# Block sums in four and three operations instead of five and four, and the first chunk's products of probabilities and v in one call

## The chip, the cores and the metric

The kernel runs on one core of a Trainium2 chip. The metric is the time of one execution in microseconds (us) of the device. TensorE (PE) multiplies matrices, with its weight loads shown apart (PEld); VectorE (DVE), ScalarE (ACT) and GpSimd (POOL) do the arithmetic around them; SyncE (SP) issues the DMAs.

## The reference

A transformer block on x of 2048 tokens by 448: layer norm, attention with 16 heads of 28 in which each token sees itself and the 255 tokens before it, a residual addition, a second layer norm, and a gated feed-forward layer of width 1792 with a second addition. All is float32.

```python
h  = x + attention(layernorm(x)) @ wo          # q.k scaled by 28**-0.5, window of 256
g  = layernorm(h) @ w_gate                     # [2048, 448] @ [448, 1792]
u  = layernorm(h) @ w_up
h2 = h + (gelu(g) * u) @ w_down
```

## The kernel before

**Precision.** Nearly every matrix operand is split in two: `to_hi` (L390, ScalarE) rounds it into a float32r part, `to_lo` (L393, VectorE or GpSimd) subtracts that part from the original. TensorE then multiplies hi by hi, hi by lo and lo by hi. L390 and L393 are helpers, so in the profile all splits have these two lines, and the tile tells them apart.

**Order of the work.** Nothing runs in the order in which it is written. Each operation is recorded with an engine, an assumed cost, a key and its dependencies (`Lists.op`); at the end `Lists.run` walks through an assumed time, takes for each engine the ready operation of the lowest key, and so fixes the order in which every engine issues its instructions. The constants at the top (LAG_T, LAG_P, EDGE, CKEY, XLATE, WLATE and so on) are offsets of keys; XADD, XADD2, XLO, XLO2, WLO and WLO2 say which of VectorE and GpSimd does a given sum or split. A changed constant can therefore move instructions anywhere.

**Attention (to about 316 us).** Tokens go in four chunks of 512, and heads in four groups of four, which makes 16 blocks B. Projections of q, k and v are L672 and L618; scores for the row maxima are L723 (with L727 on VectorE), scores again for the probabilities L798, their exponential L802 (ScalarE), the masks at the edges of the window L817 (GpSimd, `select`). `attend` (L826) multiplies v with the probabilities, in four column tiles of TensorE (L836); its matmuls are issued without a break, per call. A block has six tiles m of 128 keys, of which the first chunk (c = 0, blocks 0 to 3) has the last four. Lines 1653 to 1657 call it twice per block, with tiles (0, 1, 2) and (3, 4, 5), and in the first chunk (2, 3) and (4, 5). The output projection is L894, its addition L897.

**Feed-forward (from about 316 us to the end).** The first three column pairs of w_gate and w_up (CL = 3) are multiplied directly (L1131, L1143). The others go by Winograd's scheme, which makes a two-by-two block product of seven block products instead of eight, at the price of sums of blocks of the weights and of the tokens. Contraction blocks are 192 rows (three times 64) and lie in the two halves of 64 partitions, "sides" 0 and 1, so that two products run at once in the two row halves of TensorE (L1333, `both`). PRODUCT (L924) says at which side and slot the operands of a product lie; slots 0 to 2 hold sums, slot 3 plain blocks. The results are added up and gated at L1339 to L1361, and the product with w_down is L1407, added to the residual at L1424.

`weight_set(n)` (L1177) brings one weight matrix of a pair: DMAs, sums of blocks on GpSimd into the scratch tile xn (`sum_`, all at L1202), then hi and lo splits into the slots. There are 18 sets. `tokens_x(cp, ...)` (L994) does the same for the tokens, once for each half cp of the tokens, in three parts k of 64 rows: seven loads, a `fill`, four sums (L1041, L1044, L1047, L1050) into scratch tiles, then splits. In both halves L1044 is on GpSimd and the others on VectorE.

With a the blocks of a weight matrix, the five sums of a set are, on the sides named: a21 + a22 (both), a11 - a21 (both), the first minus a11 (side 0), the second plus a12 (side 1), and that minus a22 (side 1).

The final order of TensorE in the feed-forward stage is a chain in the written order (`queued`); sums and splits have only their keys.

Of the kernel before, what the change touches and what calls it, by code (L numbers as in the profile page):

```python
# [32 lines left out]
LAG_T = 5.0  # L33
VLAST = (-26, -21, 18, 28)
ELAST = 7
LAG_P = 15.5
LAG_V = 10.5
EDGE = 12
WIN = 9
# [3 lines left out]
CWL = 175  # L43
LATER = 4
ALONE = 5
CKEY = (214, 262)
CWKEY = (266, 222, 262, 330)
CHOLD = (10, 13, 12, 13)
X0KEY = 1330
XTIME = (6, 7, 8)  # L50
WFIRST = 1310
WLO2 = ('dve', 'dve', 'dve', 'pool')
XADD2 = ('dve', 'pool', 'dve', 'dve')
XLO2 = ('dve', 'dve', 'dve', 'pool', 'dve')
XLATE = 125
XSTEP = 60
HASTE = 300
OUTK = 80
WLATE = 110
UNIT = 100  # L60
XADD = ('dve', 'pool', 'dve', 'dve')
XLO = ('pool', 'dve', 'dve', 'dve', 'dve')
WLO = ('dve', 'pool', 'dve', 'dve')
DKEY = 284
# [5 lines left out]
LNLATE = 300  # L70
PKL = 2
LN1 = (-20, -14, 39, 128)
LN2 = (152, 260)
VKEY = (-27, -23, 17, 33)
# [177 lines left out]
def block_kernel(ctx: ExitStack, tc, x, wqk_in, wv_in, wo_in, gu_in, rest_in, cw_in, down_in, out):  # L252
# [4 lines left out]
    op = L.op  # L257
# [5 lines left out]
    def f(ap):  # L263
        return ap.bitcast(F32)
# [659 lines left out]
    PRODUCT = {1: (0, 0), 6: (0, 1), 7: (0, 2), 4: (0, 3), 2: (1, 0), 5: (1, 1), 3: (1, 2)}  # L924
# [69 lines left out]
    def tokens_x(cp, key, parts):  # L994
# [16 lines left out]
        def loads_x(k0, n):  # L1011
            for l, slot, side, c, row in ((1, 2, 0, c2, 192), (1, 1, 0, c2, 0), (1, 1, 1, c2, 0), (1, 0, 0, c1, 0),
                                          (1, 0, 1, c1, 192), (0, 1, 1, c1, 0), (1, 3, 0, c1, 192)):
                load(l, slot, side, c, row, k0, n)
# [20 lines left out]
        for k in parts:  # L1035
            key = key0 + (0 if cp else XSTEP * k)
            loads_x(k, 1)
            fill(k, 1, c2, 192 + 64 * k)
            if k < 2:
                fill(k, 2, 2 * cp + k, 384)  # L1040
            arith((XADD, XADD2)[cp][0], 512, key + 1, lambda e, k=k: e.tensor_tensor(  # L1041
                scratch(1, 0), f(area(1, 2, k, 0)), f(area(1, 1, k, 0)), op=OP.subtract),
                [*xtok(cp, 1, 2, k, 0), *xtok(cp, 1, 1, k, 0), *held(1)[1:]], held(1)[:1])
            arith((XADD, XADD2)[cp][1], 512, key + 1, lambda e, k=k: e.tensor_tensor(  # L1044
                scratch(0, 1), f(area(1, 1, k, 1)), f(area(0, 1, k, 1)), op=OP.subtract),
                [*xtok(cp, 1, 1, k, 1), *xtok(cp, 0, 1, k, 1), *held(0)[1:]], held(0)[:1])
            arith((XADD, XADD2)[cp][2], 512, key + 1, lambda e, k=k: e.tensor_tensor(  # L1047
                scratch(0, 0), scratch(1, 0), f(area(1, 0, k, 0)), op=OP.add),
                [*xtok(cp, 1, 0, k, 0), *held(1), *held(0)[1:]], held(0)[:1])
            arith((XADD, XADD2)[cp][3], 512, key + 1, lambda e, k=k: e.tensor_tensor(  # L1050
                scratch(2, 0), f(area(1, 3, k, 0)), scratch(0, 0), op=OP.subtract),
                [*xtok(cp, 1, 3, k, 0), *held(0), *held(2)[1:]], held(2)[:1])
            split(2, k, 2, 1)
            split(1, k, 2, 0)
            split(3, k, 2 if k < 2 else 0, 2)
            split(0, k, 2)
# [120 lines left out]
    def weight_set(n, key):  # L1177
# [28 lines left out]
        sum_(0, SE, 2, lambda: at(0, 1, 2), lambda: at(0, 2, 2), OP.add, wtok(n, 0, 1, 2) + wtok(n, 0, 2, 2))  # L1206
        sum_(384, SG, 2, lambda: at(0, 0, 2), lambda: at(0, 1, 2), OP.subtract, wtok(n, 0, 0, 2) + wtok(n, 0, 1, 2))
        sum_(0, SE, 0, sc(0, 0), lambda: at(0, 0, 0), OP.subtract, wtok(n, 0, 0, 0))
        sum_(384, SG, 1, sc(384, 1), lambda: at(1, 0, 1), OP.add, wtok(n, 1, 0, 1))
        sum_(384, SG, 1, sc(384, 1), lambda: at(0, 2, 1), OP.subtract, wtok(n, 0, 2, 1))  # L1210
# [410 lines left out]
    for c in range(CS):  # L1621
# [17 lines left out]
        for g in range(NG):  # L1639
# [13 lines left out]
            for half in ((0, 1, 2), (3, 4, 5)) if c else ((2, 3), (4, 5)):  # L1653
# [130 lines left out]
```

## Time and profile before

| | |
|---|---|
| median of 3 runs | 711.2 us (709.17 to 713.15) |
| the profiled execution | 710.19 us |
| its span, first to last instruction | 708.5 us |
| mean granted clock of TensorE | 0.998 |
| POOL L1202, sums of weights | 54 of 64x384, 36 of 128x384, 18 of 64x128 |
| L836, products with v | 352 matmuls, in the trace x704 |

A row of instructions in the profile reads: line, engine, operation, output tile <- input tiles, shapes and count; then busy time and the mean of one in ns, and then the idle time of the engine ahead of them with what ended it. In the timeline the first two numbers are the start and the duration in us. A row of the table by stretch has, for PE, PEld, DVE, ACT and POOL in this order, the busy time and the number of instructions, and then TensorE's granted clock as a share of full speed, the DMA share and GB/s. A row of waits has the total in us, how many times, and the longest.

### The profile page before, as it was taken

What the parts mean: (1) busy time and instruction counts of PE and PEld (TensorE: products, weight loads), DVE (VectorE), ACT (ScalarE), POOL (GpSimd) and SP (SyncE); (2) the same over time, 40 slices, a digit from 0 to 9 for tenths busy, and PEclk for the clock granted to TensorE, in tenths of its full rate; (3) what the DMA queues carried; (4) which work ended last, traced back from release to release, by engine and by line L of the source; (5) the groups of instructions that cost most, each with busy time, mean ns of one, the idle gap of its engine ahead of it and who ended that gap; (6) DMA issues with size and microseconds to landing.
All of it is one profiled execution on the core that took longest, in us unless ns stands there. A gap on an engine that the chain in (4) does not pass through costs nothing.

```text
span 708.5 us, 15457 instructions
## 1 busy us (share of the span) xinstructions
PE 695.2 (98%) x5544; PEld 587.3 (83%) x5544; DVE 534.5 (75%) x1228; ACT 414.7 (59%) x911; POOL 318.6 (45%) x431
## 2 busy tenths in 40 slices
PE   8999999999999999999999999999999999999997
PEld 7887788787888887778788798888899888898996
DVE  7977778888697879927586789986745966877764
ACT  7748576866686666866545455645434545546431
POOL 5613563644464346441354767633403456556100
PEclk9999999999999999999999999999999999999999
DMA  8997777887877677306885765504303553443102
GB/s 309 279 285 225 255 184 184 207 248 171 233 200 229 201 204 181 118 8 150 214 230 164 219 183 174 147 5 139 89 1 125 175 180 113 137 153 87 42 15 104
DMA packets 104692, 116.26 MB, mean 164 GB/s; under 512 B 44632, under 2 KB 82392, under 8 KB 104040
## 3 DMA queue, kind: packets, MB, share of 16 engines
q1 hardware_dynamic: 104472, 115.17, 56.5%
q8 instruction: 43, 0.70, 0.4%
q14 instruction: 33, 0.27, 0.1%
q10 hardware_dynamic: 144, 0.11, 0.0%
HBM read 84.97 MB, written 44.47 MB: 183 GB/s over the span
## 4 chain that ended last, share of the span: by engine, by line
PE 89%; DVE 6%; ACT 2%; issue 1%; DMA 1%; POOL 1%; DVEq 0%; ACTq 0%
PE bank L1333 24%; PE bank L1407 17%; PE bank L672 9%; PE bank L798 7%; PE bank L723 7%; PE bank L1131 7%; PE bank L836 6%; PE bank L894 5%; PE bank L618 5%; PE bank L1143 2%; DVE xT L393 1%; DVE hres L1424 1%; DVE proj L393 1%; DVE v L1343 1%; PE bank L448 0%
## 5 line engine op out<-in xcount | busy, mean ns | idle before, releaser
L727 DVE CUSTOM_DVE_ANT_0 mt<-bank,mt 128x384 bf16<-128x384 f32 (+2 forms) x256 | 127.6, 526 | 25.8 <-PE bank L723 23.0
L802 ACT ACTIVATE pp<-bank 128x384 f32<-128x384 f32 (+1 forms) x212 | 104.4, 534 | 27.1 <-PE bank L798 18.0
L817 POOL TENSOR_SCALAR_AFFINE_SELECT pp<-pp 128x512 f32<-128x512 f32 x120 | 75.8, 646 | 83.9 <-ACT pp L802 81.6
L672 PE MATMUL bank<-xT 128*128 128x512 f32 x308 | 95.4, 399 | 0.0
L1333 PE MATMUL bank<-xT,proj 64*128 64x512 f32 x735 | 94.9, 388 | 0.0
L1333 PEld LDWEIGHTS bank<-xT,proj 64*128 64x128 f32 x735 | 75.8, 184 | 9.1 <-DVE v L1343 0.3
L798 PE MATMUL bank<-rq,rk 104*128 104x384 f32 (+2 forms) x352 | 82.1, 306 | 0.5 <-ACT pp L802 0.4
L723 PE MATMUL bank<-rk,rq 84*128 84x384 f32 (+2 forms) x256 | 80.8, 340 | 0.0
L1407 PE MATMUL bank<-proj,gh 64*128 64x448 f32 x624 | 73.0, 364 | 1.5 <-ACT e L1253 0.9
L798 PEld LDWEIGHTS bank<-rq,rk 104*128 104x128 f32 x352 | 58.9, 189 | 15.0 <-ACT pp L802 4.5
L1407 PEld LDWEIGHTS bank<-proj,gh 64*128 64x128 f32 x624 | 61.3, 186 | 7.8 <-ACT e L1253 1.7
L1424 DVE TENSOR_TENSOR hres<-bank,hres 128x448 f32<-128x448 f32 (+1 forms) x113 | 62.7, 609 | 5.5 <-PE bank L1407 5.5
L1253 ACT ACTIVATE e<-bank 1x1 f32<-1x1 f32 x139 | 21.8, 157 | 74.9 <-PE bank L1407 52.7
L672 PEld LDWEIGHTS bank<-xT 128*128 128x128 f32 x308 | 55.8, 189 | 7.2 <-DVE proj L393 0.5
L1202 POOL TENSOR_TENSOR xn<-proj 128x384 f32<-128x384 f32 (+1 forms) x36 | 34.1, 952 | 56.1 <-DMA proj<-gu 36.0
L723 PEld LDWEIGHTS bank<-rk,rq 84*128 84x128 f32 x256 | 47.0, 189 | 9.8 <-issue 1.9
L393 DVE TENSOR_TENSOR proj<-proj 128x448 fp32r<-128x448 f32 (+2 forms) x42 | 34.2, 820 | 24.5 <-ACT proj L390 23.9
L1333 PE MATMUL bank<-xo,proj 64*128 64x512 f32 x366 | 49.6, 399 | 1.2 <-ACT e L1253 1.0
L390 ACT ACTIVATE rq<-bank 8x512 fp32r<-8x512 f32 x64 | 37.6, 588 | 21.3 <-PE bank L754 20.2
L618 PE MATMUL bank<-proj,xT 128*128 128x448 f32 (+1 forms) x220 | 48.9, 333 | 0.0
L836 PE MATMUL bank<-pp,v 128*29 128x384 f32 (+2 forms) x704 | 45.2, 388 | 0.0
L1333 PEld LDWEIGHTS bank<-xo,proj 64*128 64x128 f32 x366 | 38.5, 189 | 7.2 <-ACT e L1253 1.6
(177 smaller groups left out, 1429.5 us busy)
## 6 DMA issues: line engine op xcount, KB each, us to landing
rk<-k SPq DMA_DIRECT2D x44, 336.0 KB
rq<-q SPq DMA_DIRECT2D x32, 336.0 KB
gu<-in_gu_dram SPq DMA_DIRECT2D x18, 480.0 KB
proj<-gu SPq DMA_DIRECT2D x24, 288.0 KB
q<-proj SPq DMA_DIRECT2D x12, 448.0 KB
proj<-down SPq DMA_DIRECT2D x22, 224.0 KB
proj<-gu SPq DMA_DIRECT2D x24, 192.0 KB
k<-proj SPq DMA_DIRECT2D x9, 448.0 KB
```

The source lines that it names most:

```text
L618: op("pe", mm(224 * n), 0.29 if n == 1 else 0.38, key + a / 16, lambda a=a, h=h, wb=wb, xb=xb: nc.tensor.matmul(bank[b.k][:, 0:224 * n], x ...
L672: op("pe", mm(512) + 0.002, 0.403, key, lambda a=a, h=h, wb=wb, xb=xb: nc.tensor.matmul(bank[b.k], wqk[m][:, h, wb, :], xT[:, xb, cc * 128 ...
L723: nc.tensor.matmul(bank[b.k][:, o:384], rq[u][0:3 * DH, j, i * 128:i * 128 + 128], rk[u][0:3 * DH, j, m0 * 128:(i + 3) * 128], start=True, ...
L727: nc.vector.tensor_tensor_reduce(junk[s % 2][:, o:384], bank[b.k][:, o:384], mask[:, o:384], 1.0, -BIG, OP.add, OP.max, mx[:, i, j:j + 1])
L798: nc.tensor.matmul(bank[b.k][:, n * i:n * i + n], rk[u][0:104, j + i, m * 128:m * 128 + 128], rq[u][0:104, j + i, lo * 128:(hi + 1) * 128] ...
L802: nc.scalar.activation(pp[:, j:j + G, o * 128:o * 128 + n], bank[b.k][:, 0:G * n].rearrange("p (g t) -> p g t", g=G), AF.Exp, scale=SCALE)
L817: nc.gpsimd.affine_select(a, a, pattern=[[0, 4], [-cm, 128]], compare_op=op_, fill=0.0, base=0, channel_multiplier=cm)
L836: nc.tensor.matmul(bank[b.k][32 * j:32 * j + DH + 1, lo * 128:(hi + 1) * 128], v[:, at_v(4 * c - 2 + m), 4 * g + j, :], pp[:, j, at[m] * 1 ...
L1131: nc.tensor.matmul(bank[banks[side ^ ph].k], cwbuf[n % 4][0]()[HALF[side], o:o + 128], carea(c, xl, j, side), start=not ph and not j and n ...
L1333: nc.tensor.matmul(bank[b.k], w, xarea(u.cp, xl, xs, side)[:, xk], start=p in (1, 2, 5) and not k and not t, stop=t == 2, tile_position=(6 ...
L1407: nc.tensor.matmul(bank[banks[q].k][:, 0:D], h[oh][0]()[HALF[x], q * 128:q * 128 + 128], d[wh][0]()[HALF[x]], start=not ph and not y and n ...
L1424: op("dve", 0.07 + w * 0.463 / D, 0.163 + w * 0.463 / D, key, lambda: nc.vector.tensor_tensor(hres[:, t, c0:c0 + w], bank[b.k][:, c0:c0 + ...
```

## The change

The sums of blocks are formed in another sequence. For the weights: a11 - a21 (both sides), a22 minus that (both sides), a12 minus that (side 1), and a21 + a22 (side 1): four sums. For the tokens, the first difference is taken over both sides at once, which replaces two sums. On side 1 slots 1 and 2 change places, and so do the places of products 5 and 3. `attend` is called once per block in the first chunk. Many constants of keys and engines are different too; the input arrays and their layout are the same.

```diff
-LAG_T = 5.0
-VLAST = (-26, -21, 18, 28)
-ELAST = 7
-LAG_P = 15.5
+LAG_T = 7.5
+VLAST = (-30, -1, 22, 50)
+ELAST = 3
+LAG_P = 17.5
-EDGE = 12
-WIN = 9
+EDGE = 8
+WIN = 7
-CWL = 175
+CWL = -50
-CKEY = (214, 262)
-CWKEY = (266, 222, 262, 330)
-CHOLD = (10, 13, 12, 13)
+CKEY = (226, 290)
+CWKEY = (278, 234, 226, 312)
+CHOLD = (10, 13, 11, 13)
-XTIME = (6, 7, 8)
-WFIRST = 1310
-WLO2 = ('dve', 'dve', 'dve', 'pool')
-XADD2 = ('dve', 'pool', 'dve', 'dve')
-XLO2 = ('dve', 'dve', 'dve', 'pool', 'dve')
-XLATE = 125
-XSTEP = 60
-HASTE = 300
-OUTK = 80
-WLATE = 110
+XTIME = (6, 6, 7)
+WFIRST = 1500
+WLO2 = ('pool', 'dve', 'dve', 'pool')
+XADD2 = ('pool', 'pool', 'dve', 'dve')
+XLO2 = ('dve', 'pool', 'dve', 'pool', 'dve')
+XLATE = 275
+XSTEP = 90
+HASTE = 180
+OUTK = 40
+WLATE = 250
-XADD = ('dve', 'pool', 'dve', 'dve')
-XLO = ('pool', 'dve', 'dve', 'dve', 'dve')
+XADD = ('pool', 'pool', 'dve', 'dve')
+XLO = ('dve', 'dve', 'pool', 'pool', 'pool')
-DKEY = 284
+DKEY = 400
-LNLATE = 300
+LNLATE = 330
-LN1 = (-20, -14, 39, 128)
-LN2 = (152, 260)
-VKEY = (-27, -23, 17, 33)
+LN1 = (-32, -14, 39, 132)
+LN2 = (152, 254)
+VKEY = (-36, -23, 23, 30)
...
-    PRODUCT = {1: (0, 0), 6: (0, 1), 7: (0, 2), 4: (0, 3), 2: (1, 0), 5: (1, 1), 3: (1, 2)}
+    PRODUCT = {1: (0, 0), 6: (0, 1), 7: (0, 2), 4: (0, 3), 2: (1, 0), 5: (1, 2), 3: (1, 1)}
...
-            for l, slot, side, c, row in ((1, 2, 0, c2, 192), (1, 1, 0, c2, 0), (1, 1, 1, c2, 0), (1, 0, 0, c1, 0),
-                                          (1, 0, 1, c1, 192), (0, 1, 1, c1, 0), (1, 3, 0, c1, 192)):
+            for l, slot, side, c, row in ((1, 2, 0, c2, 192), (1, 1, 0, c2, 0), (1, 2, 1, c2, 0), (1, 1, 1, c1, 0),
+                                          (1, 0, 0, c1, 0), (1, 0, 1, c1, 192), (1, 3, 0, c1, 192)):
...
-            fill(k, 1, c2, 192 + 64 * k)
+            fill(k, 0, c2, 192 + 64 * k)
...
-                scratch(1, 0), f(area(1, 2, k, 0)), f(area(1, 1, k, 0)), op=OP.subtract),
-                [*xtok(cp, 1, 2, k, 0), *xtok(cp, 1, 1, k, 0), *held(1)[1:]], held(1)[:1])
+                scratch(1, 2), f(area(1, 2, k, 2)), f(area(1, 1, k, 2)), op=OP.subtract),
+                [*xtok(cp, 1, 2, k, 2), *xtok(cp, 1, 1, k, 2), *held(1)[1:]], held(1)[:1])
             arith((XADD, XADD2)[cp][1], 512, key + 1, lambda e, k=k: e.tensor_tensor(
-                scratch(0, 1), f(area(1, 1, k, 1)), f(area(0, 1, k, 1)), op=OP.subtract),
-                [*xtok(cp, 1, 1, k, 1), *xtok(cp, 0, 1, k, 1), *held(0)[1:]], held(0)[:1])
-            arith((XADD, XADD2)[cp][2], 512, key + 1, lambda e, k=k: e.tensor_tensor(
                 scratch(0, 0), scratch(1, 0), f(area(1, 0, k, 0)), op=OP.add),
                 [*xtok(cp, 1, 0, k, 0), *held(1), *held(0)[1:]], held(0)[:1])
-            arith((XADD, XADD2)[cp][3], 512, key + 1, lambda e, k=k: e.tensor_tensor(
+            arith((XADD, XADD2)[cp][2], 512, key + 1, lambda e, k=k: e.tensor_tensor(
...
-        sum_(0, SE, 2, lambda: at(0, 1, 2), lambda: at(0, 2, 2), OP.add, wtok(n, 0, 1, 2) + wtok(n, 0, 2, 2))
         sum_(384, SG, 2, lambda: at(0, 0, 2), lambda: at(0, 1, 2), OP.subtract, wtok(n, 0, 0, 2) + wtok(n, 0, 1, 2))
-        sum_(0, SE, 0, sc(0, 0), lambda: at(0, 0, 0), OP.subtract, wtok(n, 0, 0, 0))
-        sum_(384, SG, 1, sc(384, 1), lambda: at(1, 0, 1), OP.add, wtok(n, 1, 0, 1))
-        sum_(384, SG, 1, sc(384, 1), lambda: at(0, 2, 1), OP.subtract, wtok(n, 0, 2, 1))
+        sum_(0, SE, 2, lambda: at(0, 2, 2), sc(384, 2), OP.subtract, [*wtok(n, 0, 2, 2), SG])
+        sum_(0, SE, 1, lambda: at(1, 0, 1), sc(0, 1), OP.subtract, wtok(n, 1, 0, 1))
+        sum_(384, SG, 1, lambda: at(0, 1, 1), lambda: at(0, 2, 1), OP.add, wtok(n, 0, 1, 1) + wtok(n, 0, 2, 1))
...
-            for half in ((0, 1, 2), (3, 4, 5)) if c else ((2, 3), (4, 5)):
+            for half in ((0, 1, 2), (3, 4, 5)) if c else ((2, 3, 4, 5),):
```

## The prediction

> **What bounds the kernel now.** I read the page first: the span and the busy shares of the engines.
>
> ```profile
> span 708.5 us, 15457 instructions
> PE 695.2 (98%) x5544; PEld 587.3 (83%) x5544; DVE 534.5 (75%) x1228; ACT 414.7 (59%) x911; POOL 318.6 (45%) x431
> ```
>
> TensorE is the bound. The change touches no matmul: in the order in which the built program issues its instructions, both kernels have the same number of matmuls of each kind. So it can only pay where TensorE waits, or where it is "busy" but not at its pace. To find these places I read the busy time by stretch; behind each engine stands the number of its instructions, and PE's (x..) is the one to read: matmuls that started in the stretch.
>
> ```profile
> 390.00:400.00 10.00, 8.99 (x80) 7.11 (x77) 9.02 (x13) 5.09 (x14) 8.65 (x9) 1.00 0.89 274
> 400.00:410.00 10.00, 9.38 (x70) 8.09 (x72) 6.01 (x9) 4.10 (x12) 5.52 (x6) 0.83 0.47 135
> 410.00:420.00 10.00, 10.00 (x94) 9.43 (x93) 8.08 (x13) 5.50 (x14) 6.33 (x6) 1.00 0.59 183
> 420.00:430.00 10.00, 9.21 (x83) 8.06 (x81) 9.69 (x15) 7.75 (x19) 5.71 (x7) 1.00 0.84 238
> 430.00:440.00 10.00, 9.61 (x86) 8.54 (x85) 9.89 (x11) 4.07 (x12) 8.80 (x8) 1.00 0.60 181
> 440.00:450.00 10.00, 9.93 (x89) 8.61 (x87) 10.00 (x17) 5.65 (x13) 3.59 (x4) 1.00 0.57 159
> 450.00:460.00 10.00, 9.80 (x89) 8.33 (x87) 8.74 (x16) 6.71 (x18) 9.71 (x7) 1.00 0.34 105
> 500.00:510.00 10.00, 9.51 (x86) 7.76 (x86) 7.00 (x10) 5.14 (x15) 6.40 (x7) 1.00 0.09 29
> 510.00:687.00 177.00, 177.00 (x1615) 160.90 (x1613) 124.01 (x189) 85.99 (x213) 70.11 (x73) 1.00 0.34 103
> ```
>
> The last row is the feed-forward stage undisturbed: 1615 matmuls in 177 us, 91.2 in 10 us, 0.110 us each. From 390 to 460 there are 80 + 70 + 94 + 83 + 86 + 89 + 89 = 591, where 7 x 91.2 = 639 were due. The 48 missing ones are 48 x 0.110 = **5.3 us lost**; 500 to 510 lost 5 more, 0.6 us. Whose fault the 5.3 us are is told by the waits of the weight loads (PEld, TensorE's front end) from 390 to 462 us:
>
> ```profile
> PEld bank L1333 <- ACT e L1253: 1.6, 2, 1.4
> PEld bank L1407 <- DVE proj L393: 1.3, 2, 1.0
> PEld bank L1407 <- DVE xT L393: 1.2, 1, 1.2
> PEld bank L1333 <- DVE raw L1343: 0.8, 1, 0.8
> ```
>
> These, the longest, add up to 4.9 us (total, times and longest stand in each row), and 3.3 of them are for VectorE (DVE), which is busy for 61.4 of the 70 us (its column: 9.02 + 6.01 + 8.08 + 9.69 + 9.89 + 10.00 + 8.74), 88%, with 10.00 of 10 at 440. So in this stretch alone, where the first weight sets and the second half of the tokens are summed and split while TensorE already multiplies, VectorE's queue runs late and TensorE waits for it. It runs late partly because its instructions are stretched beside GpSimd (POOL):
>
> ```profile
> 427.87 0.60 DVE L393 TENSOR_TENSOR proj<-proj 128x448 fp32r<-128x448 f32 x1
> 433.28 1.46 POOL L1202 TENSOR_TENSOR xn<-xn,proj 64x384 f32<-64x384 f32 x1
> 433.97 2.52 DVE L393 TENSOR_TENSOR proj<-proj 128x448 fp32r<-128x448 f32 x1
> 434.70 1.30 POOL L393 TENSOR_TENSOR xT<-v,xT 128x512 fp32r<-128x512 f32 x1
> ```
>
> The same subtraction takes 0.60 us in one place, and 2.52 us where two GpSimd instructions cover it: it ends at 436.49, half a microsecond after the second of them (436.00).
>
> **The change part by part.** Terms come from the rows by shape:
>
> ```profile
> L1202 POOL TENSOR_TENSOR xn<-xn,proj 64x384 f32<-64x384 f32 x36 | 42.2, 1171 | 4.5 <-DMA proj<-gu 3.0
> L393 DVE TENSOR_TENSOR proj<-xn,proj 128x384 fp32r<-128x384 f32 x22 | 14.8, 671 | 6.9 <-ACT proj L390 6.9
> L393 DVE TENSOR_TENSOR proj<-proj 128x384 fp32r<-128x384 f32 x12 | 10.9, 912 | 0.5 <-issue 0.5
> L393 DVE TENSOR_TENSOR xT<-v,xT 128x512 fp32r<-128x512 f32 x14 | 12.2, 870 | 5.5 <-ACT xT L390 5.5
> L1041 DVE TENSOR_TENSOR e<-xT 64x512 f32<-64x512 f32 x3 | 2.8, 948 | 0.0
> L1047 DVE TENSOR_TENSOR raw<-raw,xo 64x512 f32<-64x512 f32 x3 | 2.0, 677 | 0.0
> L393 POOL TENSOR_TENSOR xo<-xo 128x512 fp32r<-128x512 f32 x3 | 3.9, 1297 | 7.5 <-ACT e L1253 6.1 <-issue 1.5
> L393 POOL TENSOR_TENSOR proj<-xn,proj 128x384 fp32r<-128x384 f32 x2 | 2.3, 1142 | 0.2
> ```
>
> *Weight sums, 18 sets.* Five sums become four: one 64x384 sum of 1.17 us less per set on GpSimd, 18 x 1.17 = 21 us. It hides beside TensorE nearly everywhere, so by itself it is worth nothing at the end, but the set's last operands are ready 1.2 us sooner.
>
> *Token sums, 6 parts.* Four sums become three. VectorE did three of each four (L1041, L1047, L1050) and GpSimd one; now GpSimd does two (the first of 128 partitions, 1.3 us by the 128x512 row) and VectorE the last. VectorE loses 12 sums of 0.68 to 0.95 us, 12 x 0.81 = 9.7 us; GpSimd gains 6 of about 1.3, 8 us. The loads stay seven per part: the half that (0,1) held now goes to (1,2), and the second load of (1,1) reads the first block instead of the second. The fill goes to scratch 0, not 1. The DMA queue keeps its 560 instructions, so I price this at 0.
>
> *Splits re-dealt (XLO, XLO2, WLO2).* The issue order of the built programs moves 15 splits of 128x384, 5 of 128x512 and 2 of 64x512 from VectorE to GpSimd: 22 x 0.79 to 0.87, some 18 us more off VectorE, and 22 x 1.14 to 1.30, some 26 us onto GpSimd.
>
> *What that is in the late stretch.* I count between the same two matmuls, the first and the 425th of L1333, which the trace has from 382 to 460 us. VectorE issues 4 sums, 4 splits of 128x384 and 3 of 128x512 fewer, and two small others more: 4 x 0.81 + 4 x 0.79 + 3 x 0.87 - 1.0 = **8 us less**. GpSimd issues 6 weight sums fewer, 3 token sums, 4 splits of 128x384, 3 of 128x512 and one of 64x512 more: -7.1 + 3.9 + 4.6 + 3.9 + 1.3 = **6.6 us more**, to about 55 of 70 us from 48.3 (its column above), which still leaves it idle time. VectorE falls from 88% to about 77% there, so its queue drains. The gain is at most the 5.3 us lost. Below zero the bound is the 6.6 us that GpSimd takes on, should TensorE come to wait for GpSimd instead. I take 4 us, nearer the upper end, because two thirds of the waits above name VectorE and none names GpSimd. The pace behind a wait is part of the loss:
>
> ```profile
> 400.62 3.71 PE bank L1333 x18
> 405.76 2.09 PE bank L1333 x18
> ```
>
> The 18 matmuls after that wait took 3.71 us instead of 2.09, in the stretch whose clock was 0.83. Without the wait, 1.6 us of slow clock go with it; they are part of the 5.3. The Trainium skill, "TensorE: Matmul & The Clock Gate", section "What's actually happening", says that the clock falls to half after an idle window of about 3.4 us. By that rule the waits here, 1.4 us at most, would not slow the clock, the 1.6 us would not come back with them, and the gain would be 2.4 us instead of 4. The trace shows 0.83 at those waits all the same, so the sum goes by the row.
>
> *One call for the first chunk's products.* Blocks 0 to 3 issue L836 in one group of 32 instead of two of 16. The block that has them side by side already is the price tag:
>
> ```profile
> 63.27 2.15 PE L836 MATMUL bank<-pp,v 128*29 128x384 f32 x32
> 65.35 0.31 PE L754 MATMUL bank<-one,mhl 128*104 128x128 f32 x1
> ...
> 76.92 1.50 PE L836 MATMUL bank<-pp,v 128*29 128x384 f32 x16
> 78.34 0.62 PE L723 MATMUL bank<-rk,rq 84*128 84x384 f32 x2
> 78.89 0.86 PE L836 MATMUL bank<-pp,v 128*29 128x256 f32 x16
> 79.68 0.44 PE L723 MATMUL bank<-rk,rq 84*128 84x384 f32 x1
> 80.20 0.34 PE L723 MATMUL bank<-rk,rq 84*128 84x384 f32 x1
> 80.38 0.86 PE L672 MATMUL bank<-xT 128*128 128x512 f32 x3
> ```
>
> Side by side, start to next start is 65.35 - 63.27 = 2.08 us. Split, 79.68 - 76.92 = 2.76, less two L723 at 0.18 (80.38 - 80.20) = 2.40. So 0.32 us are saved per block; the issue order shows three blocks split before (31 such groups then, 28 now): 3 x 0.32 = **1.0 us**. The call now waits for all four tiles of probabilities, and everything on TensorE queues behind it. If the last mask of GpSimd is late, the cost is one mask per block, 0.65 us:
>
> ```profile
> L817 POOL TENSOR_SCALAR_AFFINE_SELECT pp<-pp 128x512 f32<-128x512 f32 x120 | 75.8, 646 | 83.9 <-ACT pp L802 81.6 <-PE bank L723 1.8 <-PE bank L798 0.2
> PEld bank L798 <- ACT pp L802: 4.5, 13, 0.8
> ```
>
> That is at worst 3 x 0.65 = 2 us; I take 0, since that mask is off TensorE's path unless the projections and scores between run out.
>
> *The keys.* LAG_T, LAG_P, EDGE, WIN and the other constants move matmuls of the attention part against each other. The one wait there that they could remove is the last row, 4.5 us from 60 to 316 us; they could as well double it. Bounds -4.5 and +4.5, taken as 0: the instructions are the same, and TensorE's idle share there is small.
>
> *Sum.* The profiled execution took 710.2 us, 1.7 around its span, and 1.0 below the median of the three runs (711.2). 710.2 - 4.0 - 1.0 = 705.2, which is 706.2 on the median's footing. I forecast **706 us**.
>
> **The rivals.** *A, all of it goes:* 5.3 + 0.6 (the wait at 507 us) + 1.0 + half of the 4.5 us of attention waits = 9.1, so 702. For it: VectorE is relieved on both sides of the stretch. Against: the first two rows, 390 to 410, hold 3.6 us of the loss (182 matmuls due, 150 there), and by the issue order VectorE has about the same number of instructions in them.
>
> *B, the relief is taken back by the shared access:* what leaves VectorE, 8 us, appears on GpSimd as 6.6 us, and the rest of VectorE's queue is stretched by it as at 433.97. Joint need falls by only 1.4 us; TensorE wins 1 us there and 1.0 from the merged call: 709. The Trainium skill, "SBUF — State Buffer", section "Who interferes with whom", states this rule: a VectorE instruction with two inputs in SBUF and a GpSimd instruction that reads SBUF block each other for the whole instruction. The row of 2.52 us agrees with it.
>
> *C, slower: GpSimd becomes the bound of a weight set.* Its queue holds the sums in order ahead of the splits that now follow on it; TensorE takes the set's split operands last. It decides once GpSimd's 6.6 us more no longer fit into its idle time ahead of the set's first matmul: 21.7 us idle over the stretch, but in the row 450 to 460 only 0.3. Then TensorE waits 6.6 us for GpSimd: 711.2 + 6.6 - 1.0 = 717.
>
> That the change does not do what it says is excluded: the issue order has 36 sums of 64x384 instead of 54 and 28 groups of L836 instead of 31.
>
> **How the numbers follow.** Forecast 0.46, its own range 703 to 709; A 0.15; B 0.22; C 0.17. About 0.5% (3.6 us) is what a measurement here can tell from no change, so faster means below 707.6 and slower above 714.8. The forecast's range lies below 707.6 for about 0.37 of its 0.46; with A and 0.02 of B that is 0.54 faster. Within: 0.09 + 0.20 of B = 0.29. Slower: C, 0.17. The range reaches from 699.5 (A with all of the 4.5 us) to 714.5, which leaves out most of C and little else.
>
> **What would show it.** Right: from 390 to 460 the matmuls per 10 us reach 88 to 94 in each row, the clock stays at 1.00, VectorE is below 85%, and the waits for L393 and L1343 shrink from 3.3 us to about 1; the first chunk's L836 come as x32. B: VectorE's splits grow longer (912 ns and more) and its share stays near 88%. C: waits of PEld for POOL L393 appear after 380 us. Wrong altogether: a gain or loss before 316 us of more than 2 us, which only the keys could make.

## The result, and the profile after

| | before | after |
|---|---|---|
| median | 709.87 us (707.70 to 713.42, 13 runs) | 706.87 us (704.63 to 709.14, 13 runs) |
| ratio | | 0.9955, 95% interval 0.9937 to 0.9972 |
| profiled execution, its span | 710.19, 708.5 us | 707.69, 706.0 us |
| first matmul of L1333, start | 382.01 us | 383.68 us |
| last matmul of L1333, start | 685.98 us | 683.46 us |

The change makes the kernel 3.0 us faster. In the changed kernel, line numbers in the feed-forward part are 3 or 4 lower: L1333 is L1329 there, L1407 is L1403, L1253 is L1249, L1343 is L1339, and the weight sums are L1199. I call the time from the first to the last matmul of this line the Winograd stage.

The page of the changed kernel, its span and busy shares:

```profile
span 706.0 us, 15432 instructions
PE 693.6 (98%) x5544; PEld 583.7 (83%) x5544; DVE 501.8 (71%) x1194; ACT 414.7 (59%) x911; POOL 325.5 (46%) x441
```

VectorE is busy for 32.7 us less than before (534.5), GpSimd for 6.9 us more (318.6). Where this falls is told by one row each for the Winograd stage, before and then after:

```profile
382.00:683.00 301.00, 297.44 (x2669) 263.79 (x2667) 222.45 (x335) 151.62 (x375) 144.27 (x139) 0.99 0.41 123
```

```profile
382.00:683.00 301.00, 298.89 (x2709) 262.12 (x2707) 203.03 (x320) 153.22 (x383) 144.41 (x144) 1.00 0.42 125
```

The change is visible here as a trade: in place of the saved weight sums (21 us over the whole program) GpSimd does splits and token sums, to the same 144 us, and VectorE loses 19.4 us. TensorE does 40 matmuls more in the same 301 us. They lie in the stretch of the prediction. After, by stretch, and then before for the 70 us in one row:

```profile
345.00:390.00 45.00, 42.47 (x367) 36.18 (x365) 27.58 (x47) 22.25 (x58) 25.02 (x20) 0.96 0.67 186
400.00:410.00 10.00, 9.79 (x89) 8.06 (x90) 6.84 (x12) 5.68 (x16) 5.50 (x5) 1.00 0.68 202
420.00:430.00 10.00, 8.30 (x78) 6.88 (x76) 9.43 (x14) 7.64 (x19) 8.17 (x9) 1.00 0.90 252
440.00:450.00 10.00, 10.00 (x94) 8.99 (x93) 9.42 (x15) 4.76 (x12) 6.93 (x7) 1.00 0.73 205
390.00:460.00 70.00, 68.09 (x616) 59.67 (x615) 54.03 (x81) 43.09 (x106) 52.51 (x50) 1.00 0.65 189
```

```profile
390.00:460.00 70.00, 66.93 (x574) 58.18 (x573) 61.42 (x88) 38.87 (x97) 48.32 (x42) 0.98 0.61 182
```

VectorE falls from 61.4 to 54.0 us, GpSimd rises from 48.3 to 52.5, and TensorE does 616 matmuls instead of 574. From 345 to 390, however, it does 367, where the prediction's profile has this for the same stretch:

```profile
345.00:390.00 45.00, 44.12 (x396) 36.79 (x398) 35.55 (x56) 24.44 (x65) 20.02 (x18) 1.00 0.70 191
```

So 29 matmuls fewer are recorded here, some 3 us of work, and the first product starts 1.7 us late. The weight loads' longest waits from 390 to 462 us, after:

```profile
PEld bank L1403 <- DVE xT L393: 2.1, 1, 2.1
PEld bank L1329 <- ACT e L1249: 0.6, 1, 0.6
PEld bank L1403 <- DVE hres L1420: 0.2, 1, 0.2
PEld bank L1329 <- DVE v L1339: 0.2, 1, 0.2
```

Those for proj and raw (1.3 and 0.8 us before) are gone, and that for the read L1249 has fallen from 1.6 to 0.6. One has grown, for the split xT, from 1.2 to 2.1 us. The timeline shows why: GpSimd's new token sum covers it.

```profile
426.78 1.65 POOL L1041 TENSOR_TENSOR e<-xT 128x512 f32<-128x512 f32 x1
427.23 1.75 DVE L393 TENSOR_TENSOR xT<-v,xT 128x512 fp32r<-128x512 f32 x1
429.03 0.91 PEld L1403 LDWEIGHTS bank<-proj,xT 64*128 64x128 f32 x10 [2.10 <-DVE xT L393]
```

The loss between 345 and 390 us has one place, too. The weight loads, and ScalarE in the same microseconds:

```profile
360.81 1.21 PEld L1403 LDWEIGHTS bank<-proj,xT 64*128 64x128 f32 x12 [2.84 <-ACT e L1249]
```

```profile
357.96 0.76 ACT L443 ACTIVATE v<-hres,bnve 128x448 f32<-128x448 f32 x1 [1.43 <-DMA xn<-v]
358.63 0.61 ACT L390 ACTIVATE xo<-raw 128x512 fp32r<-128x512 f32 x1
359.15 0.61 ACT L390 ACTIVATE xo<-e 128x512 fp32r<-128x512 f32 x1
359.67 1.06 ACT L1153 ACTIVATE v<-bank 128x512 f32<-128x512 f32 x2
360.62 0.34 ACT L1249 ACTIVATE e<-bank 1x1 f32<-1x1 f32 x2
```

A normalisation (L443) waits for a DMA at the head of ScalarE's queue, and the short reads L1249, which release TensorE's next accumulation, stand behind it.

### The profile page after: what moved, and what is told of

Its sections match the earlier page's. It is cut to its first block, busy times and chain, and to the rows that moved or that the text cites. A ratio compares the mean times of both kernels' runs of the same rounds, so it can differ in the third digit from the quotient of the medians.

```text
span 706.0 us, 15432 instructions
## 1 busy us (share of the span) xinstructions
PE 693.6 (98%) x5544; PEld 583.7 (83%) x5544; DVE 501.8 (71%) x1194; ACT 414.7 (59%) x911; POOL 325.5 (46%) x441
## 4 chain that ended last, share of the span: by engine, by line
PE 92%; DVE 3%; DMA 2%; ACT 1%; issue 1%; SPq 0%; POOL 0%; DVEq 0%; ACTq 0%
PE bank L1329 26%; PE bank L1403 17%; PE bank L672 9%; PE bank L798 7%; PE bank L723 7%; PE bank L1128 6%; PE bank L836 6%; PE bank L894 5%; PE bank L618 5%; PE bank L1140 2%; DMA pp<-in_wv_dram 1%; DVE hres L1420 1%; DMA xn<-v 1%; PE bank L448 0%; DMA hres<-in_x_dram 0%
## 5 line engine op out<-in xcount | busy, mean ns | idle before, releaser
L1329 PE MATMUL bank<-xT,proj 64*128 64x512 f32 x735 | 94.5, 389 | 0.0
L672 PE MATMUL bank<-xT 128*128 128x512 f32 x308 | 93.0, 399 | 0.0
L1329 PEld LDWEIGHTS bank<-xT,proj 64*128 64x128 f32 x735 | 72.9, 184 | 11.9 <-ACT e L1249 0.4
L1403 PE MATMUL bank<-proj,gh 64*128 64x448 f32 x624 | 72.2, 363 | 0.1
L1403 PEld LDWEIGHTS bank<-proj,gh 64*128 64x128 f32 x624 | 60.0, 184 | 6.9 <-ACT e L1249 1.2
L1249 ACT ACTIVATE e<-bank 1x1 f32<-1x1 f32 x139 | 21.8, 157 | 69.6 <-PE bank L1403 45.7
L1199 POOL TENSOR_TENSOR xn<-proj 128x384 f32<-128x384 f32 (+2 forms) x36 | 34.5, 961 | 46.5 <-DVE e L393 19.0
L1329 PE MATMUL bank<-xo,proj 64*128 64x512 f32 x366 | 48.1, 389 | 0.2 <-ACT e L1249 0.2
L393 DVE TENSOR_TENSOR proj<-proj 128x448 fp32r<-128x448 f32 (+2 forms) x32 | 24.0, 761 | 31.1 <-ACT proj L390 28.8
L1403 PE MATMUL bank<-proj,xT 64*128 64x448 f32 x312 | 38.4, 368 | 4.4 <-ACT e L1249 2.5
```

The source lines that it names most:

```text
L672: op("pe", mm(512) + 0.002, 0.403, key, lambda a=a, h=h, wb=wb, xb=xb: nc.tensor.matmul(bank[b.k], wqk[m][:, h, wb, :], xT[:, xb, cc * 128 ...
L1329: nc.tensor.matmul(bank[b.k], w, xarea(u.cp, xl, xs, side)[:, xk], start=p in (1, 2, 5) and not k and not t, stop=t == 2, tile_position=(6 ...
L1403: nc.tensor.matmul(bank[banks[q].k][:, 0:D], h[oh][0]()[HALF[x], q * 128:q * 128 + 128], d[wh][0]()[HALF[x]], start=not ph and not y and n ...
```

## The experiments

Three theories were open. **T1**: VectorE's relief is the gain, and it comes from the splits that were dealt to GpSimd. **T2**: the saved sums are the gain. **T3**: the merged call and the keys carry part of it. All ratios are to the kernel before, run beside each on the same chip: its median was 709.78 us for e1 to e4, 708.42 for e5 to e8, 709.51 for e9 and e10, and 709.20 for e11 and e12. Where two kernels stand beside different ones of these, the ratios are what to compare. In all but e5 and e6 the order of all instructions is fixed as the list in `Lists.run` gives it, and `move(a, b)` then puts one recorded operation ahead of another (with True: behind it).

| kernel | median us (lowest to highest, runs) | ratio, 95% interval | first product | Winograd stage |
|---|---|---|---|---|
| before, changed kernel | 709.87, 706.87 | 0.9955 (0.9937 to 0.9972) | 382.0, 383.7 | 304.0, 299.8 |
| e1_merge_alone | 710.45 (708.35 to 713.02, 12) | 1.0004 (0.9984 to 1.0023) | 386.7 | 302.1 |
| e2_norm_behind | 705.35 (704.75 to 705.68, 6) | 0.9939 (0.9920 to 0.9958) | 380.3 | 300.8 |
| e3_norm_and_sum | 704.51 (703.78 to 705.59, 6) | 0.9930 (0.9911 to 0.9950) | 381.5 | 299.8 |
| e4_splits_back | 711.32 (709.28 to 715.07, 12) | 1.0022 (1.0005 to 1.0039) | 382.4 | 304.2 |
| e5_keys_alone | 719.38 (716.86 to 721.71, 5) | 1.0146 (1.0121 to 1.0172) | 386.0 | 309.1 |
| e6_sums_alone | 716.06 (714.62 to 719.20, 6) | 1.0101 (1.0078 to 1.0125) | 392.1 | 302.9 |
| e7_before_split_behind | 708.24 (707.25 to 710.35, 11) | 0.9994 (0.9980 to 1.0007) | 382.3 | 301.5 |
| e8_split_first | 704.87 (703.74 to 705.51, 6) | 0.9943 (0.9924 to 0.9962) | 379.7 | 299.8 |
| e9_sum_doubled | 712.66 (710.89 to 715.14, 12) | 1.0042 (1.0025 to 1.0059) | 381.8 | 305.0 |
| e10_token_sum_back | 706.88 (705.82 to 707.61, 6) | 0.9948 (0.9928 to 0.9969) | 382.4 | 299.7 |
| e11_fills | 714.78 (712.12 to 715.25, 6) | 1.0065 (1.0040 to 1.0089) | 384.1 | 307.0 |
| e12_read_first | 705.82 (705.29 to 705.94, 5) | 0.9945 (0.9923 to 0.9966) | 379.7 | 301.4 |

The last two columns come from each kernel's timeline: the start of the first matmul of L1333 (L1329) and the time to the start of the last. They are of one execution each.

**The merged call alone**, in the order of the kernel before.

```diff
+    att = L.all["att"]
+    for b in range(1, 4):
+        move(att[2 * b], att[2 * b + 1])
```

> The kernel before with its own issue order, in which only the first of the two calls with products of v is moved down to the second in blocks 1 to 3. If the switch between two groups of L836 is paid in full (0.32 us per block, as predicted), the time falls by 1.0 us and the attention part ends 1.0 us sooner. If a later wait of the attention part takes the gain back, the last L894 starts where it did (320.4 us) and the time is unchanged within 0.3 us.

It gains nothing. TensorE's timeline of e1 at the place that the prediction priced:

```profile
77.72 0.62 PE L723 MATMUL bank<-rk,rq 84*128 84x384 f32 x2 [0.45 <-DVE mx L727]
78.27 2.15 PE L836 MATMUL bank<-pp,v 128*29 128x384 f32 x32
80.35 0.44 PE L723 MATMUL bank<-rk,rq 84*128 84x384 f32 x1
```

The products do take 80.35 - 78.27 = 2.08 us now instead of 2.40. But the two score matmuls that had lain between the halves now come first, and wait 0.45 us for VectorE's maxima. Over the whole of attention these waits rise by 1.1 us, before and then in e1, about what the three blocks should have saved:

```profile
PEld bank L723 <- DVE mx L727: 0.2, 1, 0.2
```

```profile
PEld bank L723 <- DVE mx L727: 1.3, 3, 0.8
```

In this profile the last group of L894 starts at 321.61 us, 1.2 us later than before.

**One wait of ScalarE in the changed kernel**: the second-last normalisation goes behind the two reads that it held up.

```diff
+    move(L.ops[2867], L.ops[2979], True)
```

> The changed kernel with its own issue order, in which one instruction of ScalarE, the second-to-last norm of the second layer norm (L443, which waits for DMAs to leave its output buffer), is moved behind the two small reads (L1249) for which TensorE waited 2.84 us at 358 us. Theory: the gain of the relief was given back in part by this new wait; then the wait goes, the matmuls from 345 to 390 us rise from 367 to about 395, and the time falls by 2.5 to 3 us, to about 704. Rival: TensorE is held at that place by something else that is late too (the tokens' splits or a DMA), and the time falls by less than 1 us.

The median falls to 705.35, and six runs lie within 1 us, where the thirteen of the changed kernel lie within 4.5. The weight loads of e2 at that place:

```profile
358.77 1.11 PEld L1403 LDWEIGHTS bank<-proj,xT 64*128 64x128 f32 x12 [0.74 <-ACT e L1249]
```

The wait falls from 2.84 to 0.74 us, and the matmuls from 345 to 390 us rise from 367 to 397, as expected. Of the 2.5 to 3 us that were expected, the medians show 1.5 and the ratios 1.1, and the intervals of the ratios overlap: the place of the loss is shown, its price only roughly.

**And the token sum** at 427 us in addition, moved behind GpSimd's next small split.

```diff
     move(L.ops[2867], L.ops[2979], True)
+    move(L.ops[3202], L.ops[3270], True)
+    move(L.ops[3199], L.ops[3270], True)
```

> As the run with the norm moved, and besides the last 128x512 token sum on GpSimd (L1041, at 427 us) stands behind the next small split on GpSimd. Theory of the shared access: the split on VectorE beside it (xT<-v, 1.75 us) falls to about 0.7 us, TensorE's wait there (2.1 us) to about 1, and the time by another 1 us. Rival: the split is stretched by whatever GpSimd does there or waits for something else, so 1.7 us stay; or the sum, now later, delays the tokens of the second half and makes a wait after 440 us.

VectorE's timeline of e3, and then TensorE's:

```profile
425.07 0.68 DVE L393 TENSOR_TENSOR xT<-v,xT 128x512 fp32r<-128x512 f32 x1
```

```profile
425.80 1.28 PE L1403 MATMUL bank<-proj,xT 64*128 64x448 f32 x10 [0.61 <-DVE xT L393]
```

The split takes 0.68 us instead of 1.75 without the GpSimd sum beside it, and the wait of TensorE's matmuls falls from 1.70 to 0.61. The time falls by 0.8 us, less than can be told apart from e2 (the intervals overlap). This version, at 704.51, has the lowest median of all.

**The splits given back**, in the changed kernel's order: VectorE does 22 more than there, and a slot of xo goes the other way.

```diff
+                  real=(("pool", "dve", "dve", "dve", "dve"), ("dve", "dve", "dve", "pool", "dve"))[cp][slot])
...
+                real=("dve", "pool" if n < 3 else "dve", "dve", "pool" if n > 2 else "dve")[slot])
```

> The changed kernel with its own issue order, in which the 22 splits that had gone to GpSimd are done by VectorE again (and the three that went the other way by GpSimd); the sums, the merged call and every place in the order stay as changed. Theory: relief of VectorE in the late stretch is the gain, so from 390 to 460 us the matmuls fall back from 636 towards 591 and the time rises by 2 to 4 us. Rival: the shorter sums and the other order made the gain; then the time stays within 1 us.

The ratio rises by 0.0067 over the changed kernel's, 4.8 us: all of the gain, and more than the 2 to 4 us expected. The waits of e4 from 390 to 462 us, its worst stretch, and the 70 us in one row:

```profile
PEld bank L1407 <- DVE xT L393: 2.5, 1, 2.5
PEld bank L1407 <- DVE hres L1424: 1.5, 3, 1.1
```

```profile
430.00:440.00 10.00, 10.00 (x80) 8.40 (x78) 5.07 (x9) 4.62 (x14) 7.95 (x8) 0.83 0.56 166
390.00:460.00 70.00, 66.86 (x585) 58.72 (x584) 53.34 (x83) 40.45 (x100) 44.08 (x43) 0.98 0.66 186
```

TensorE waits for VectorE again, and does 585 matmuls instead of 616. T2 as "the sums alone" does not hold: e4 has them and gains nothing. T1 holds in that the new dealing is needed in this order, but not as a matter of load: VectorE is busy for 53.3 us of these 70, no more than in the changed kernel (54.0). Over the whole program, VectorE (511.0 us) and GpSimd (295.8 us) are both less busy in e4 than in the kernel before (534.5 and 318.6), and e4 is still slower. So how busy the engines are does not explain the 4.8 us. The order of e4 was worked out for the new dealing, and that a departure from it costs time of its own is not excluded.

**The keys and engines alone**, with the old sums and the two calls (the diff is the constants of the change, without XADD and XADD2).

```diff
-WLO2 = ('dve', 'dve', 'dve', 'pool')
+WLO2 = ('pool', 'dve', 'dve', 'pool')
...
-XLO2 = ('dve', 'dve', 'dve', 'pool', 'dve')
+XLO2 = ('dve', 'pool', 'dve', 'pool', 'dve')
```

> The kernel before (five and four sums, two calls of attend per block) with the changed kernel's keys and its dealing of the splits to engines; the token sums stay on the engines that they had, since there is one more of them. Theory (VectorE's relief between 390 and 460 us by the re-dealt splits is the gain, and the sums that were saved only make room on GpSimd for it): some of the 4.4 us that giving the splits back cost is kept, but GpSimd now has the re-dealt splits and the old sums too, 18 x 1.17 = 21 us of them. About 708, between 706.5 and 710, and waits of the weight loads for POOL L393 or for sums appear after 380 us. Rival 1 (the sums are the gain, the keys nothing): 710, no wait for POOL. Rival 2 (without the room, GpSimd becomes the bound of a weight set): 713 or more.

It is 10 us slower. Rival 2 has the time, but no wait of the weight loads names GpSimd. The first product comes 4.0 us later than in the kernel before, and then there is one long wait for VectorE:

```profile
477.07 0.57 PEld L1333 LDWEIGHTS bank<-xT,proj 64*128 64x128 f32 x4 [4.31 <-DVE xT L393]
```

```profile
460.00:470.00 10.00, 9.61 (x89) 7.85 (x88) 9.32 (x9) 5.92 (x16) 9.77 (x9) 1.00 0.01 2
470.00:480.00 10.00, 6.11 (x45) 5.30 (x43) 7.95 (x14) 1.39 (x3) 0.73 (x1) 0.79 0.01 3
480.00:490.00 10.00, 10.00 (x82) 9.67 (x80) 2.66 (x4) 3.84 (x9) 0.00 (x0) 0.87 0.28 77
```

In the 10 us up to 470 GpSimd is busy for 9.77 and VectorE for 9.32, and the last token operand is ready only at 477. So the new dealing alone is not enough: under these keys the re-dealt splits without the saved sums make the kernel slower. The keys were made for fewer sums, so this run does not tell the missing room from the unfitting order.

**The sums and the merged call alone**, with the keys and engines of before (the same constants the other way round, and XADD = XADD2 = ('pool', 'dve', 'dve')).

> The changed kernel (four and three sums, one call of attend) with the keys and engines of the kernel before; of the three token sums GpSimd does the first, VectorE the others. Theory (the re-dealt splits are the gain): as without them, 709 to 711, VectorE above 85% from 390 to 460 us except for the token sums that it has lost (12 x 0.81 us, of which four in that stretch), so at best 1 us below the kernel before. Rival (the sums saved are the gain): 707. Second rival (an order worked out for other keys falls apart): above 712, with waits spread over the whole feed-forward stage.

7.6 us slower, as the second rival had it, but not in its place. The Winograd stage is 302.9 us long; attention is the place. Its waits, and the last group of the output projection in e6:

```profile
PEld bank L723 <- DVE mx L727: 7.1, 13, 1.8
```

```profile
329.65 5.13 PE L894 MATMUL bank<-proj,ohl 128*128 128x448 f32 x24
```

Before, that wait was 0.2 us and the last group of L894 began at 320.39. With the old keys the merged call makes the scores for the maxima come too close behind VectorE's work on the maxima. In the changed kernel, with the merged call and the new constants, the group begins at 320.63; which of the constants avoids the 9 us is not shown. With the new constants and two calls, in e5, it begins at 321.45. So the call and the keys belong together. Under the new keys the merged call may be worth up to 0.8 us, but the profiles with the changed kernel's attention lie between 320.58 and 321.20 themselves.

**ScalarE's wait in the kernel before**: a split that waits for a load goes behind the reads.

```diff
+    move(L.ops[2850], L.ops[2987], True)
```

> The kernel before in its own order, with one thing moved: the 64x512 token split on ScalarE (L390, near 358 us), which waits for a load, goes behind the next reads of the gate (L1253) that TensorE waits for. In one profiled run of that order these reads came 2.2 us late. Theory (the wait of ScalarE for a load is in both kernels, and whether it shows varies from execution to execution; it is what spreads the times of the kernel before over 707 to 714): median 708.5 to 709.5, 0.5 to 1.3 us below the kernel before, and less spread. Rival (the wait belongs to the changed order alone): 709.8, the spread as it was.

No gain that can be told: 708.24 beside 708.42, and the interval of the ratio holds the theory's 0.5 us as well as the rival's nothing, so the run does not decide. The rival's condition is wrong in any case: in e1, which has the old order but for the merged call, TensorE waits 2.2 us for these reads, while the profiles of before and of e7 have no such wait there. The profile of e7 is useful all the same, as a second one of the old order. The stretch in which the prediction saw the clock at 0.83:

```profile
400.00:410.00 10.00, 9.84 (x90) 9.16 (x92) 8.62 (x12) 4.69 (x14) 7.19 (x8) 1.00 0.51 146
390.00:460.00 70.00, 67.54 (x596) 60.60 (x594) 63.82 (x90) 40.84 (x102) 50.98 (x44) 1.00 0.66 184
```

The clock stayed at 1.00, and 596 matmuls were done in the 70 us. e1, the old order too, has 596 as well. The 574 of the profiled execution were a worse case.

**A further move on VectorE** on top of e3.

```diff
+    move(L.ops[3343], L.ops[3317])
```

> The order with the norm's split and the token sum moved, and in addition on VectorE the split of the gated product (L393, xT, near 425 us) ahead of the split of the down weights that stands in front of it (0.6 us). Theory (TensorE's wait of 1.0 us there is this split's place in VectorE's queue): 704.0, half a microsecond below that order, and the wait near 425.8 falls to 0.4. Rival (the reads behind it take the wait over): 704.5, the wait comes back within 5 us.

The wait near 425 us is gone (in e8 the largest of its kind is 0.5 us), and the time is the same as e3's, as the rival had it. The next wait, 5 us on, is for ScalarE, 0.7 us instead of 0.5.

**The saved sum as work again**: the changed kernel, with the last 64x384 sum of each set done twice.

```diff
-            arith("pool", w, key + 1, lambda e: e.tensor_tensor(xn_m[HALF[side], o:o + w], a(), b(), op=what), rd, [tok])
+            arith("pool", w, key + 1, lambda e: [e.tensor_tensor(xn_m[HALF[side], o:o + w], a(), b(), op=what) for _ in range(times)], rd, [tok])
```

> The changed kernel in its own order, where the last 64x384 sum of each weight set is done twice in a row on GpSimd (the second time with the same result): the fifth sum is back as work, 18 x 1.17 = 21 us, and nothing else differs. Theory (the sums that were saved are the room in GpSimd's queue that the re-dealt splits need): the sets of the stretch from 380 to 460 us are late, the time rises by 1 to 4 us over the changed kernel, to 707.5 to 710.5 by a kernel before at 709.8, and TensorE waits for ACT or POOL operands of w or proj. Rival (GpSimd had room for both, 23% idle in that stretch): within 0.7 us of the changed kernel, 0.9945 to 0.9965 of the kernel before, and the new dealing alone is the gain.

The ratio rises by 0.0087 over the changed kernel's, 6.2 us: twice the gain of the whole change, and more than the theory's 1 to 4. The mark that the theory named is not there: no wait of the weight loads from 380 us on names GpSimd, nor an operand of w or proj from ScalarE. The page of e9, and then one group of VectorE's splits, in e9 and in the changed kernel:

```profile
PE 695.2 (98%) x5544; PEld 585.9 (83%) x5544; DVE 516.7 (73%) x1194; ACT 414.5 (58%) x911; POOL 345.4 (49%) x459
```

```profile
L393 DVE TENSOR_TENSOR proj<-xn,proj 128x384 fp32r<-128x384 f32 x22 | 16.5, 756 | 11.2 <-ACT proj L390 7.9 <-ACT e L1249 3.2
```

```profile
L393 DVE TENSOR_TENSOR proj<-xn,proj 128x384 fp32r<-128x384 f32 x22 | 13.4, 615 | 7.5 <-ACT proj L390 5.5 <-ACT e L1249 1.5 <-POOL xn L1199 0.4
```

GpSimd is busy for 19.9 us more, and VectorE for 14.9 us more with exactly the same 1194 instructions: the same 22 splits take 756 ns instead of 615. The profiles of e2, e3, e8 and e12, also with 1194 instructions, have VectorE at 505.4 to 508.0 us, so 9 to 15 us of this come from the doubled sums. So 20 us of sums on GpSimd give VectorE back a quarter to nearly half of the 32.7 us that the change had taken off it. Whether this is by stretching the instruction beside them, or by delaying what follows on GpSimd, is what e11 asks.

**A token sum given back** to VectorE.

```diff
+                [*xtok(cp, 1, 2, k, 2), *xtok(cp, 1, 1, k, 2), *held(1)[1:]], held(1)[:1], real="dve")
```

> The changed kernel in its own order, with the first token sum (L1041, 128x512, six times) back on VectorE. Theory (VectorE's load between 390 and 460 us is what TensorE waits for): VectorE takes three of them there, 3 x 0.7 to 0.95 us, and the time rises by 1 to 2 us, to 0.998 of the kernel before. Rival (the sum on GpSimd stretches a split of VectorE by 1 us, so it cost what it saved): the same as the changed kernel or up to 0.8 us below, as when that sum was moved away from the split.

The same as the changed kernel: the rival. That this sum went to GpSimd contributes nothing that can be told. It also shows that not every departure from the changed order costs time.

**Fills in place of the doubled sums**: as long on GpSimd, but without reading SBUF.

```diff
+                  ahead=lambda: [nc.gpsimd.memset(xn_m[HALF[side], o:o + w], 0.0) for _ in range(fills)])
```

> The changed kernel in its own order; where the last 64x384 sum of each weight set was done twice, it is done once, and in place of the other time GpSimd writes zeros three times to the place that the sum then fills: about the same time on GpSimd (some 3 x 0.35 us, by the 32x1536 fill of 1.38 us), but without reading SBUF. It tells why the doubled sums cost 6 us. Theory 1 (GpSimd's own queue: the set's operands are later by the length of the extra work): as dear as the doubled sums, 1.002 to 1.006 of the kernel before. Theory 2 (sums on GpSimd stretch VectorE's instructions beside them, and TensorE waits for VectorE): VectorE's busy time stays near 502 to 507 us (517 with the doubled sums), and the time stays near that of the changed kernel, 0.994 to 0.998.

As dear as the doubled sums (7.8 us by the ratios, the intervals overlap), for 22.4 us of fills, as theory 1 had it. Here too no wait of the weight loads names GpSimd. GpSimd's row and VectorE's at a place where they meet:

```profile
390.57 1.38 POOL L1200 MEMSET xn<- 64x384 f32 x3
```

```profile
390.72 0.55 DVE L393 TENSOR_TENSOR proj<-proj 128x384 fp32r<-128x384 f32 x1
```

A fill does not stretch the split beside it (0.55 us). The Trainium skill, "SBUF — State Buffer", section "Who interferes with whom", says so as well: an instruction of VectorE with two inputs in SBUF contends with a GpSimd instruction that reads SBUF, not with one that only writes. Yet VectorE's busy time rises to 514.8 us here too. The extra work pushes GpSimd's own sums and splits later, to where VectorE does its own splits; the same split of gh, in the changed kernel and in e11, where GpSimd's instructions beside it follow:

```profile
444.14 1.78 DVE L393 TENSOR_TENSOR gh<-v,gh 128x512 fp32r<-128x512 f32 x1
```

```profile
445.87 3.43 DVE L393 TENSOR_TENSOR gh<-v,gh 128x512 fp32r<-128x512 f32 x1
```

```profile
446.23 1.28 POOL L1041 TENSOR_TENSOR e<-xT 128x512 f32<-128x512 f32 x1
447.47 1.28 POOL L393 TENSOR_TENSOR xT<-v,xT 128x512 fp32r<-128x512 f32 x1
```

The split ends at 449.30, 0.55 us after the second of them.

For VectorE's busy time it therefore counts when GpSimd reaches its reading instructions, not only how many of them there are.

**A split that waits, behind two reads**, on top of e3.

```diff
+    move(L.ops[2839], L.ops[3029], True)
+    move(L.ops[2838], L.ops[3029], True)
```

> The order with the norm's split and the token sum moved, and in addition the 64x512 token split on ScalarE (L390, xo, near 373 us, where it waits 1.7 us for a VectorE sum), with the GpSimd split that follows from it, goes behind the two reads (L1249) that TensorE waits for at 375 us. Theory (each wait of TensorE that is made by a waiting instruction in front of such a read goes when the read is moved ahead, and pays what it lasted): 703.5, 0.9 us below that order. Rival (the split is then late itself, and the first products by Winograd's scheme wait for it at 381 us): 704.5 or more, with a wait for xo near 381 us.

No gain: 705.82, and its interval overlaps that of e3. The wait at 375 us is gone and the first product comes at 379.7, but the stage is 1.6 us longer. The rival's wait for xo near 381 us is not seen.

## Why the prediction was right, and where it was not

The forecast was 706, the median 706.87. The sum had 4.0 us from VectorE's relief, 1.0 from the merged call, and nothing from the rest. It forecast a gain of 5.0 us, and 3.0 came. That the time was missed by only 0.9 us is luck: the sum started from 711.2, the median of three runs, which lies 1.3 us above that of thirteen.

*The place* was right. From 390 to 460 us VectorE fell by 7.4 us (8 were forecast), its share to 77%, GpSimd rose by 4.2 (6.6 were forecast), and the waits for the splits of proj went. The waits for L393 and L1343 together fell from 3.3 to 2.3 us, not to about 1. Of the marks that were to show it, the clock stayed at 1.00 and the matmuls reached 89 to 96 in six of the seven rows; 420 to 430, with its wait of 2.1 us, had 78. Attention is unchanged in length, with the first chunk's products in one group, as in this row of the changed kernel:

```profile
66.75 2.14 PE L836 MATMUL bank<-pp,v 128*29 128x384 f32 x32
```

*The reason* given, VectorE's share of busy time, is not enough: e4 has the same share (53.3 of 70 us, 76%) and no gain. What the runs show is that both parts, the new dealing and the room on GpSimd, are needed in this order.

*The size* of 4 us agrees with the two profiles, for a poor reason. Adding seven rows of 10 us counted the matmuls that lie across their ends twice; the single row has 574, not 591, so the loss was (638 - 574) x 0.110 = 7.0 us, not 5.3, and of this (616 - 574) x 0.110 = 4.6 came back. But e1 and e7 show 596 in the old order, so 22 of the 42 were a disturbance of that one execution (the stretch at 0.83). The usual relief is (616 - 596) x 0.110 = 2.2 us there, and 1.7 to 4.2 us over the Winograd stage (301.5 to 304.0 in the three profiles of the old order, 299.8 in the changed kernel's one; with single operations moved, e2, e3, e8 and e12 have 299.8 to 301.4).

*"By itself it is worth nothing at the end"*, said of the saved weight sum, is right as far as it goes: e4 has the saving and no gain. The 0 that it became in the sum failed. Put back, one sum per set costs 6 us (e9). Giving the splits back costs 4.8 (e4). Each undoes more than the whole gain, so the two parts are not terms of a sum: in this order the gain needs both. That the order was made for both, and suits neither alone, may be part of these prices. The waits named VectorE and never GpSimd, and the prediction took this for independence; in e9 and e11 they do not name GpSimd either, and yet its extra work is paid in full. VectorE's own instructions last as long as GpSimd's beside them allow.

*The merged call's 1.0 us* failed: e1 has 1.0004. The 0.32 us are saved in the block where they were priced, and the score matmuls moved ahead wait 1.1 us more for VectorE's maxima. The changed kernel's attention ends no sooner than before.

*The keys, taken as 0*: their order puts the normalisation ahead of the reads, and e2 puts the cost at 1.1 to 1.5 us, within the uncertainty. In all five profiles of the changed order without that move (the changed kernel, e4, e9, e10, e11) this wait is 2.1 to 3.1 us. It is not theirs alone: of the three profiles of the old order, e1 has 2.2 us there, behind a split that waits for a load. In attention the new constants offset what the merged call would cost under the old keys (e6): the last group of L894 begins at 320.39 before and at 320.63 after.

*Rival B*, the shared access, happened at one place where TensorE waited for it: the split of 1.75 us beside the new token sum, which ends 0.55 us after that sum does. e3 got 0.8 us there, within the uncertainty. As an account of the whole it was too dark. *Rival C* did not occur in the changed kernel. In e5, with 21 us more of sums, GpSimd has hardly any idle time from 452 to 470 us and the kernel is slower, but the long wait is for a token split on VectorE and not for a weight set on GpSimd.

What stays open is how e9's and e11's 6 to 8 us divide between late operands and stretched splits, and how much of the prices of e4, e9 and e11 is the unfitting order. No run here separates them.

## What to carry to other kernels

Two engines that feed TensorE in the same stretch are not separate terms: work on one can delay or stretch the other's even where no wait names it, so ask of each saved instruction what it makes room for. To price a part of a change, put it back as work in the changed order, as with the doubled sum, and put back beside it a part that should cost nothing, as with the token sum: an order suits what it was made for. And before a stretch of one profile is priced, compare it with a second execution: here a third of the loss that was measured did not come again.

## What the runs showed of the hardware

The clock's dips do not follow from the length of the wait before them alone. After waits of at most 1.4 us it was 0.83 in the profile before, and at the same place of the same order 1.00 in e7, where the wait 2 us ahead of it was 0.2 instead of 1.0 us. With a wait of 3.0 us it was 1.00 in e10, while the same wait in the changed kernel, 2.8 us, has 0.96 in the same 45 us; e10's wait (total, times, longest; L1405 is the same line there), and the stretch in which it lies:

```profile
PEld bank L1405 <- ACT e L1251: 4.3, 4, 3.0
```

```profile
345.00:390.00 45.00, 42.26 (x379) 35.18 (x377) 32.53 (x50) 22.77 (x59) 23.26 (x19) 1.00 0.72 193
```

After the 4.31 us of e5 it was 0.79 and 0.87 in two rows of 10 us. The dips have their size in common. Of 10 us, 0.83 is a loss of 1.7 us (before, and e4 from 430 to 440); of 45 us, 0.96 is 1.8; and e5 has 2.1 + 1.3 = 3.4, twice as much. The Trainium skill, "TensorE: Matmul & The Clock Gate", section "What's actually happening", has the clock fall after an idle window of about 3.4 us; e5 and e10 agree with it, the profile before, the changed kernel and e4 do not.

The other surprise is the spread of the times: 4.5 us between the fastest and the slowest run of the changed kernel, 0.9 us in e2, where one instruction of ScalarE stands elsewhere. The clock goes with it: the changed kernel's runs with a mean clock of 0.996 or 0.997 took 706.87, 708.47, 708.69 and 709.14 us, the other nine 704.63 to 707.69, and in e2 none is below 0.998. One dip of 1.7 us lowers the mean over 706 us by 0.002. Whether the DMA's arrival near 358 us decides on such a dip is not shown: e10, with the instruction in its old place, has 1.8 us between its six runs.
